# Early expert lists cut at three, five and seven counted groups, and weight stores as a task of their own

## The chip, the cores and the metric

The kernel runs on one core of a Trainium2 chip. The metric is the device time of one execution in microseconds (us). The core has five engines, each with its own queue in program order: TensorE (PE, its weight loads PEld), VectorE (DVE), ScalarE (ACT), GpSimd (POOL) and SyncE (SP), which here only issues DMAs. "Granted clock" is the share of full speed that TensorE was given, as the profile shows it.

## The reference

Three layers follow each other on 14336 tokens of 192 numbers (4 sequences of 3584).

```
out = sum over k of softmax(weight)[h, k] * x[t - 6 + k]        # 8 heads of 24, 7 taps
# first mixture: only tokens with out @ w_skip > 0
e = argmax(out @ w_gate);  g = softmax(out @ w_gate)[e]
x1 = out + g * (relu(out @ w1[e]) @ w2[e])                      # w1: 8 x 192 x 1024, w2: 8 x 1024 x 192
# second mixture: all tokens, a gate bias by modality
e2 = argmax(x1 @ w_gate2 + bias[modality]);  y = g2 * (relu(x1 @ w1b[e2]) @ w2b[e2])
```

The result is y. Each token goes through one expert of the first mixture or none, and one of the second.

## The kernel before, in words

**Phase 1** (`Phase1`, lines 669 to 840) makes the 7-tap sum and the gate scores. Tokens lie in 128 tiles of 112, in 8 groups of 16 tiles. A step v (line 821) does one head of one group's convolution, the transposes and gate matmuls of older pieces, and twice a *tick* of the task lists. `fin` (line 776) turns a group's scores into expert codes and metadata and stores the group's rows (values as two float16 halves) to `rows` in DRAM (line 805). There are 64 convolution steps and 12 more that finish.

**Counting and lists.** `route_a` (line 392) runs for each group when its codes are there: it counts tokens by expert (a scan `cuma`, a matmul with `tri` and `ones`, many small GpSimd operations), gives each token a place, and writes the token numbers of each place by one-hot matmuls (`oa`, `ob`). Each expert has `SB` = 7 blocks of 128 places. After `GA` = 4 groups the places of the first `EA` = 4 experts in `SA` = 3 blocks each are closed (line 434: the running base is raised to 3 * 128), and the sum so far is copied to the list `la` (line 484, index tile `idxa`). After 8 groups the list `ls` (`idxs`) is complete. Tokens beyond 7 blocks stay in `code` and are routed into 6 more blocks (`l1`), tokens of the second model that skip the first into list `lb` (`idxB`) and the rest into `l2`; that is `route` (line 585) with `ranks`, `qsl` and `invert`.

**Blocks.** `Ffn.run` (line 1017) goes through jobs. A block of 128 rows is gathered by GpSimd (an indirect DMA by the list), transposed by a DMA on SP, multiplied by the first weights (`mm1`, in two halves, into banks read by ScalarE as `hh` and by VectorE as `hlo`), and one job later by the second (`mm2`). Blocks of the first model add a residual (GpSimd, `xs`) and end in `x2a`/`x2s` on VectorE. `order` (line 1171) is: the first 12 blocks from `la` (experts 0 to 3, three each), then the rest of experts 1, 2, ..., 7, then 0, 44 blocks from `ls`; then 6 of `l1`. Jobs of the second model follow, mostly two to a set of weights.

**Weights.** `prep` (line 289) scales one expert's weights after another: squares of both matrices (before the first blocks by matmuls, later by ScalarE into `sa`), a sum over partitions by a matmul, a power of two `wsc`, then high halves by ScalarE and low halves by VectorE into `w1b`/`w2b` (first model, 3 buffers, `buf`) or into the one buffer `o` (second model), and stores to `s1a`, `s2a`, `s1b`, `s2b`. Two *lanes* (`LANES`, line 36) run it: lane 0 from phase 1 on, lane 1 from the time when phase 1's pools are given back (`late_pools`, line 1242). `guard` (line 1181) holds a scaling until its buffer is out of use (`step` at or beyond the last early or full block of expert e - 3, plus 2) or until `o` is free.

**What sets the order.** All work beside the blocks is written as Python generators; `yield n` means "go on in n ticks". `Tasks.tick` advances them, and `bg(i, pt)` (line 1301) calls it at four places of each block i: `tk` (counting and routes) twice while i < 12 and `ls` isn't ready, else once; `tkw` (the lanes) once; `tk2` (block maxima and scaling, `scale2`, line 942) once. While phase 1 has steps left, `bg` also does one. The order in which the generators issue is the order in each engine's queue, so a number after `yield` sets how far an instruction stands from what it waits for. At block 56 whatever is left in the lists is issued at once (`drain`).

Of the kernel before, what the change touches and what calls it, by code (L numbers as in the profile page):

```python
# [7 lines left out]
F32 = mybir.dt.float32  # L8
# [21 lines left out]
GA = 4  # L30
EA = 4
SA = 3
# [3 lines left out]
LANES = [(0, e) for e in range(E)] + [(1, 7)], [(1, e) for e in range(7)]  # L36
# [78 lines left out]
class Moe:  # L115
# [173 lines left out]
    def prep(self, ws, pool, pq, dst, guard, done, es, lane, lag, pace, free, busy, first, early):  # L289
# [22 lines left out]
        for n, (q, e) in enumerate(es):  # L312
            (wt, wr), w2t = nxt
            if early():
                for i, vs in enumerate(((wt,) * 8 + (wr[0:64],) * 8, (w2t,) * 12)):
                    for k, v in enumerate(vs):
                        c = k % 8 if i == 0 else k
                        v = v.bitcast(BF16)[:, c * 256 + 1:c * 256 + 256:2]
                        nc.tensor.matmul(g[:, i, :], v, v, start=(k == 0), stop=(k == len(vs) - 1))
                    yield 1  # L320
                yield 2
                dg = pq.tile([128, 512], F32, name="dg", bufs=1)[:, 0:256].rearrange("p (i c) -> p i c", i=2)
                nc.vector.tensor_tensor(dg, g, self.identf.unsqueeze(1).to_broadcast([128, 2, 128]), ALU.mult)
# [16 lines left out]
            yield 1  # L340
# [41 lines left out]
            yield 2 + q  # L382
            nc.sync.dma_start(ws[q][2][e], o1)
            yield 2 + q
            nc.sync.dma_start(ws[q][3][e], o2.bitcast(I32))
            yield 2 + q
            if q:
                free[0] = None
            if not last:
                yield max(1, lag() - 3 * (2 + q))  # L390

    def route_a(self, g, code, pool, ob, res):
# [41 lines left out]
        if g == GA - 1:  # L434
            nc.gpsimd.tensor_scalar(base[:, 0:EA], base[:, 0:EA], float(SA * 128), None, ALU.max)
# [47 lines left out]
        if g == GA - 1:  # L483
            self.finish("a", e, S, res["a"], 0)
# [4 lines left out]
    def finish(self, tag, ei, S, res, base, lp=None):  # L489
        nc = self.nc  # L490
        lp = lp or self.cp
        va = lp.tile([128, S], F32, name="va" + tag)
        nc.vector.tensor_scalar(va, ei, 0.0, None, ALU.is_gt)
        idx = lp.tile([128, S], I32, name="idx" + tag)
        if base:
            nc.vector.scalar_tensor_tensor(ei, va, float(base), ei, ALU.mult, ALU.add)
        nc.vector.tensor_scalar(idx, ei, 127.0, None, ALU.add)
        res.update(idx=idx, va=va)

    def ranks(self, code, pool, lag, r, wait=6):  # L500
# [6 lines left out]
        of = oh.rearrange("p c t -> p (c t)")  # L507
        nc.vector.tensor_tensor_scan(cum.rearrange("p c t -> p (c t)"), of, of, 0.0, ALU.add, ALU.max)
# [31 lines left out]
    def invert(self, S, q, sl, pool, ob, tag, res, lp, lag, base=0, val=None):  # L540
# [8 lines left out]
        for h in range(nb + 1):  # L549
            if h < nb:  # L550
# [5 lines left out]
                yield lag // 2  # L556
# [28 lines left out]
    def route(self, code, nst, tag, pool, ob, res, base=0, lag=1, S=None, np=0, lp=None, val=None):  # L585
# [49 lines left out]
        nc.vector.tensor_reduce(pos, cum.rearrange("p c t -> p t c"), AX.X, ALU.add)  # L635
        yield 1
# [32 lines left out]
class Phase1:  # L669
# [50 lines left out]
    def conv(self, g, h):  # L720
        nc, m = self.nc, self.m
        if h == 0:
            self.hl[g] = self.px.tile([TP, GT, RW], F16, name="hlx", bufs=1) if g == GA - 1 else self.p3.tile([TP, GT, RW], F16, name="hl", bufs=4)
# [119 lines left out]
class Ffn:  # L843
# [98 lines left out]
    def scale2(self, x2, mt, nb):  # L942
# [10 lines left out]
        yield 1  # L953
# [186 lines left out]
def build(tc, x, cw, m1w1, m1w2, mod, bias2, m2w1, m2w2, wgs, out):  # L1140
    with ExitStack() as ctx:
# [12 lines left out]
        la, ls, l1, lb, l2, lr = {}, {}, {}, {}, {}, {}  # L1154
# [25 lines left out]
        def lane(k):  # L1180
# [7 lines left out]

            return m.prep(ws, w["pw2"] if k else pw, pq, dst, guard, (d1, d2), LANES[k], k, lambda: 8 if k else 8 if late() else 14, lambda: 1 if late() else 3, owner, conv, 8 if k else 26, lambda: not late())

        def routes():
# [5 lines left out]
            while k < NSA:  # L1197
# [5 lines left out]
                k += n  # L1203
                yield 1
# [23 lines left out]
        while "idx" not in la:  # L1228
            if phase1() is None:
                tk.tick()  # L1230
# [11 lines left out]
        def late_pools():  # L1242
# [11 lines left out]
            tk.add(routes())  # L1254

# [36 lines left out]
        jobs = [mk(1, la if k < EA * SA else ls, e * SB + j, rows[0:GA * GT * 128 + 128, :] if k < EA * SA else rows, col=k, b=buf[e]) for k, (e, j) in enumerate(order)]  # L1292
# [8 lines left out]
        def bg(i, pt):  # L1301
# [35 lines left out]
            if i < n2:  # L1337
                for _ in range(2 if i < EA * SA and "idx" not in ls else 1):
# [71 lines left out]
```

## Time and profile before

| | us |
|---|---|
| median of 3 runs (lowest to highest) | 1015.85 (1015.10 to 1019.68) |
| profiled execution: time | 1015.87 |
| profiled execution: span of instructions | 1014.1 |
| PE busy | 929.5 (92%) |
| VectorE busy | 633.5 (62%) |
| GpSimd busy | 524.5 (52%) |
| ScalarE busy | 501.7 (49%) |
| mean granted clock of TensorE | 0.965 |

Busy time is the sum of instructions on an engine, so a share of 92% says nothing of where the other 8% are; the views by stage do. The first matmul of the first block runs at 139.79 us, the first matmul of the second model at 485.32 us. Times in rows are microseconds from the start of the span unless marked ns.

### The profile page before, as it was taken

The numbers are of one execution on the slowest core, as the hardware profiler recorded it, in microseconds if no ns is written. First come the engines' busy times: TensorE is split into PE (matmuls) and PEld (weight loads), VectorE is DVE, ScalarE is ACT, GpSimd is POOL, SyncE is SP. The second block draws the span as 40 slices with busy tenths as digits, with TensorE's granted clock in tenths as the row PEclk, the third lists the DMA queues.
The fourth block names the chain that finished last, engine by engine and source line by source line (L and its number), as shares of the span: only waits on it lengthen the run. The fifth ranks groups of instructions, "written<-read, shape, count | busy, mean of one in ns | idle before, by whom it ended". The sixth has DMA issues, their size and how long they took to land. (4 is left out here: it accounts for less than half of the span.)

```text
span 1014.1 us, 29393 instructions
## 1 busy us (share of the span) xinstructions
PE 929.5 (92%) x11174; PEld 865.0 (85%) x11174; DVE 633.5 (62%) x1716; ACT 501.7 (49%) x937; POOL 524.5 (52%) x1027
## 2 busy tenths in 40 slices
PE   5998969999898789998899999999999999999994
PEld 3666668899898789997799988998898999999994
DVE  5699976999989988983455555558633333333331
ACT  2786743656686555642455555543233333333331
POOL 4055788454344243334287776854355555555532
PEclk9999958999999899998999999999999999999997
DMA  8495778858899598579733334332275222233231
GB/s 292 147 319 204 238 237 210 228 177 219 232 251 264 129 304 241 170 240 259 257 81 108 98 88 117 99 112 67 55 257 164 72 76 73 74 75 75 74 96 47
DMA packets 109142, 165.49 MB, mean 163 GB/s; under 512 B 80975, under 2 KB 86073, under 8 KB 103232
## 3 DMA queue, kind: packets, MB, share of 16 engines
q1 hardware_dynamic: 94368, 134.02, 43.2%
q0 software_dynamic: 13920, 28.87, 12.0%
q8 instruction: 90, 1.47, 0.6%
q10 hardware_dynamic: 704, 0.63, 0.2%
q14 instruction: 60, 0.49, 0.2%
HBM read 181.56 MB, written 58.42 MB: 237 GB/s over the span
## 5 line engine op out<-in xcount | busy, mean ns | idle before, releaser
L70 PEld LDWEIGHTS <-w1b 128*128 128x128 f16 x4840 | 372.0, 99 | 40.3 <-issue 13.9
L70 DVE SCALAR_TENSOR_TENSOR ws<-bank,ws 128x512 f16<-128x512 f32 x220 | 151.9, 691 | 256.6 <-ACT ws L70 255.3
L70 PE MATMUL bank<-xp,w1b 128*128 128x256 f16 x2200 | 263.9, 273 | 4.3 <-DMA w1b<-s1b 2.6
L70 PE MATMUL bank<-w2b,ws 128*128 128x192 f16 x2640 | 239.1, 246 | 0.0
L70 PEld LDWEIGHTS <-ws 128*128 128x128 f16 (+2 forms) x2724 | 224.9, 98 | 2.3
L70 POOL DMA_INDIRECT out_dram<-u,si x114 | 115.2, 1011 | 167.8 <-ACT u L70 111.3
L70 ACT ACTIVATE ws<-bank 128x512 f16<-128x512 f32 x220 | 130.7, 597 | 119.5 <-PE bank L70 118.8
L70 PE MATMUL bank<-xt,w1b 128*128 128x128 f16 x2640 | 167.1, 223 | 10.4 <-DVE hlo L70 7.1
L70 PE MATMUL bank<-w2b,hh 128*128 128x192 f16 x1056 | 143.2, 252 | 4.6 <-DMA w2b<-s2a 4.6
L70 PE MATMUL bank<-w2b,hlo 128*128 128x192 f16 x528 | 132.8, 252 | 0.0
L70 ACT ACTIVATE hh<-bank 128x512 f16<-128x512 f32 x132 | 77.4, 591 | 103.4 <-PE bank L70 99.5
L70 DVE SCALAR_TENSOR_TENSOR hlo<-bank,hh 128x512 f16<-128x512 f32 x132 | 89.9, 685 | 49.8 <-ACT hh L70 49.5
L70 ACT ACTIVATE u<-bank,c 128x192 f32<-128x192 f32 x114 | 48.0, 421 | 146.5 <-PE bank L70 121.3
L70 POOL DMA_INDIRECT gt<-rows,idxs x44 | 50.0, 1136 | 131.8 <-issue 118.3
L70 PEld LDWEIGHTS <-hh 128*128 128x128 f16 x1056 | 97.3, 102 | 5.4 <-issue 4.8
L70 POOL DMA_INDIRECT gt<-rows,idx x64 | 63.5, 992 | 27.0 <-issue 15.0
L70 POOL DMA_INDIRECT gt<-rows,idxB x56 | 55.8, 997 | 27.3 <-issue 12.2
L70 PE MATMUL bank<-xg,band 128*112 128x384 f32 x128 | 58.8, 549 | 4.5 <-DVE hl L70 4.3
L70 POOL TENSOR_TENSOR xs<-gt 128x128 f32<-128x128 f16 x124 | 54.9, 467 | 5.5 <-DVE x2s L70 3.6
L70 PE MATMUL bank<-ob,oa 128*128 128x56 f16 (+2 forms) x446 | 50.0, 263 | 8.2 <-DVE ob L70 7.2
L70 ACT COPY xtb<-bank 128x672 f16<-128x672 f16 x64 | 46.0, 721 | 17.3 <-PE bank L70 17.0
L70 PEld LDWEIGHTS <-hlo 128*128 128x128 f16 x528 | 52.9, 100 | 0.3
(256 smaller groups left out, 1210.6 us busy)
## 6 DMA issues: line engine op xcount, KB each, us to landing
w1b<-s1b SPq DMA_DIRECT2D x59, 1024.0 KB
w2b<-s2b SPq DMA_DIRECT2D x59, 768.5 KB
ws<-in_moe_w_dram SPq DMA_DIRECT2D x16, 768.0 KB
xg<-in_x_dram SPq DMA_DIRECT2D x7, 1536.0 KB
rows<-hl SPq DMA_DIRECT2D x7, 1386.0 KB
ws<-in_moe_w_dram SPq DMA_DIRECT2D x16, 512.0 KB
ws<-in_moe_w_dram SPq DMA_DIRECT2D x32, 256.0 KB
s1a<-w1b SPq DMA_DIRECT2D x8, 1024.0 KB
```

What stands on the lines that cost most here:

```text
L70: r = f(*args, **kw)
```

## The change

The early list becomes three lists. `CUTS` names for each the groups counted and the range of blocks of an expert that it closes: after 3 groups blocks 0 and 1 of experts 0 to 2, after 5 groups blocks 2 and 3, after 7 groups blocks 4 and 5. So 18 blocks come first, six from each list, and of experts 1, 2 and 0 one block each is left for `ls`. Lane 0 scales expert 0 of the second model after expert 2 of the first; lane 1 has six experts. The two stores of a scaling become a generator `keep`, which after the start is a task of its own (`side`). Several `yield` numbers, the order of the squares, and the size of three VectorE operations (scan and two-part reduction) change. `tk` is ticked once a block's place while phase 1's pools live, twice from then to the last early list, then once.

```diff
-GA = 4
-EA = 4
-SA = 3
+CUTS = (3, 0, 2), (5, 2, 4), (7, 4, 6)
+EA = 3
+SA = CUTS[-1][2]
+NA = EA * SA
-LANES = [(0, e) for e in range(E)] + [(1, 7)], [(1, e) for e in range(7)]
+LANES = [(0, 0), (0, 1), (0, 2), (1, 0)] + [(0, e) for e in range(3, E)] + [(1, 7)], [(1, e) for e in range(1, 7)]
@@ prep
-                sa = pq.tile([128, 4], F32, name="sa", bufs=1)
-                for k, v in enumerate((wt, w2t[:, 0:4 * D], wr, w2t[:, 4 * D:])):
+                sa = pq.tile([128, 4], F32, name="sa", bufs=2)
+                for k, v in ((0, wt), (2, wr), (1, w2t[:, 0:4 * D]), (3, w2t[:, 4 * D:])):
...
-                    yield 2
+                    yield 2 if k < 3 else 5
...
             nc.vector.tensor_scalar(sc, sc, 2.0 ** 30, 2.0 ** FT, ALU.min, ALU.mult)
-            yield 1
+            yield 1 if early() else 3
...
-            yield 2 + q
-            nc.sync.dma_start(ws[q][2][e], o1)
-            yield 2 + q
-            nc.sync.dma_start(ws[q][3][e], o2.bitcast(I32))
-            yield 2 + q
-            if q:
-                free[0] = None
-            if not last:
-                yield max(1, lag() - 3 * (2 + q))
+            st = self.keep(ws, q, e, o1, o2, free)
+            if early():
+                for w in st:
+                    yield w
+                if not last:
+                    yield max(1, lag() - 3 * (2 + q))
+            else:
+                side.add(st)
+                if not last:
+                    yield 4
+    def keep(self, ws, q, e, o1, o2, free):
+        nc = self.nc
+        yield 2 + q
+        nc.sync.dma_start(ws[q][2][e], o1)
+        yield 2 + q
+        nc.sync.dma_start(ws[q][3][e], o2.bitcast(I32))
+        yield 2 + q
+        if q:
+            free[0] = None
@@ route_a
-        if g == GA - 1:
-            nc.gpsimd.tensor_scalar(base[:, 0:EA], base[:, 0:EA], float(SA * 128), None, ALU.max)
+        for n, _, b in CUTS:
+            if g == n - 1:
+                nc.gpsimd.tensor_scalar(base[:, 0:EA], base[:, 0:EA], float(b * 128), None, ALU.max)
...
-        if g == GA - 1:
-            self.finish("a", e, S, res["a"], 0)
+        for k, (n, _, _) in enumerate(CUTS):
+            if g == n - 1:
+                self.finish(f"a{k}", e, S, res["a"][k], 0, va=False)
@@ ranks
-    def ranks(self, code, pool, lag, r, wait=6):
+    def ranks(self, code, pool, lag, r, wait=4):
...
-        nc.vector.tensor_tensor_scan(cum.rearrange("p c t -> p (c t)"), of, of, 0.0, ALU.add, ALU.max)
+        for c in (0, 4):
+            of = oh[:, c:c + 4].rearrange("p c t -> p (c t)")
+            nc.vector.tensor_tensor_scan(cum[:, c:c + 4].rearrange("p c t -> p (c t)"), of, of, cum[:, 3, T - 1:T] if c else 0.0, ALU.add, ALU.max)
+            if not c:
+                yield 1
@@ invert
-                yield lag // 2
+                yield (lag - 1) // 2
@@ route
-        nc.vector.tensor_reduce(pos, cum.rearrange("p c t -> p t c"), AX.X, ALU.add)
-        yield 1
+        h = (T + 1) // 2
+        for a, b in ((0, h), (h, T)):
+            nc.vector.tensor_reduce(pos[:, a:b], cum[:, :, a:b].rearrange("p c t -> p t c"), AX.X, ALU.add)
+            yield 1
@@ scale2
         nc.vector.scalar_tensor_tensor(mt[:, :, 0], ef, 0.5, mt[:, :, 0], ALU.mult, ALU.mult)
-        yield 1
+        yield 4
@@ build
-        order = [(e, j) for e in range(EA) for j in range(SA)]
+        order = [(e, j) for _, a, b in CUTS for e in range(EA) for j in range(a, b)]
         order += [(e, j) for e in (*range(1, E), 0) for j in range(SA if e < EA else 0, SB)]
-        last = lambda e: max(i for i, o in enumerate(order) if o[0] == e and (e or i < SA))
+        last = lambda e: max(i for i, o in enumerate(order) if o[0] == e and (e or i < NA))
...
-        while "idx" not in la:
+        while "idx" not in la[0]:
...
+            tk2.add(kept())
...
-                for _ in range(2 if i < EA * SA and "idx" not in ls else 1):
+                for _ in range(2 if "x" in w and "idx" not in la[-1] else 1):
                     tk.tick()
```

`kept` is the copying of `va` for the complete list, taken out of `routes` and run in `tk2`. The jobs of an early list read `rows` only up to the groups it was counted from.

## Rows read from the trace of the kernel before

**Rows 1.** Busy time by stage: window, length, PE, PEld, DVE, ACT, POOL, clock, DMA, GB/s.
```profile
139.80:200.30 60.50, 52.49 (x634) 51.49 (x635) 43.81 (x113) 28.07 (x49) 42.85 (x118) 0.83 0.87 241
...
200.30:311.00 110.70, 104.53 (x1574) 103.68 (x1572) 100.50 (x273) 72.74 (x133) 49.09 (x92) 1.00 0.79 219
...
311.00:365.00 54.00, 41.73 (x565) 40.40 (x563) 52.32 (x141) 30.64 (x54) 19.32 (x34) 0.91 0.77 224
...
365.00:447.80 82.80, 81.23 (x1147) 80.94 (x1146) 71.35 (x173) 45.64 (x83) 34.83 (x67) 1.00 0.79 222
...
447.80:485.30 37.50, 29.96 (x409) 28.86 (x406) 17.59 (x46) 10.63 (x21) 12.84 (x24) 0.90 0.90 267
...
485.30:1014.00 528.70, 503.67 (x5558) 474.38 (x5558) 234.96 (x636) 222.11 (x442) 291.31 (x478) 0.99 0.37 102
```

**Rows 2.** Timeline of PE around the first block: start, length, operation, idle time before.
```profile
136.95 1.03 PE L70 MATMUL bank<-ob,oa 128*128 128x56 f16 x8 [1.22 <-DVE ob L70]
...
139.79 4.18 PE L70 MATMUL bank<-xt,w1b 128*128 128x128 f16 x40 [1.48 <-POOL genda L70]
...
147.87 0.59 PE L70 MATMUL bank<-cuma,tri 128*128 128x8 f32 x2 [3.90 <-DVE cuma L70]
```

**Rows 3.** Timeline of POOL from the fourth list to the last count.
```profile
123.56 0.46 POOL L70 TENSOR_TENSOR cuma<-cuma,oha 128x128 f32<-128x128 f32 x1
...
129.25 1.21 POOL L70 DMA_INDIRECT gt<-rows,idxa  x1 [0.19 <-issue]
...
173.10 0.22 POOL L70 TENSOR_TENSOR code<-code,oka 128x16 f32<-128x16 f32 x1
```

**Rows 4.** Timeline of SP, 158 to 172 us; last, its waits there (total, times, longest).
```profile
162.54 0.33 SPq L805 DMA_DIRECT2D rows<-hl  x1
...
169.18 0.34 SPq L296 DMA_DIRECT2D ws<-in_moe_w_dram  x1
...
SPq L296 <- DMA rows<-hl: 3.4, 1, 3.4
```

**Rows 5.** Timeline of DVE: results of blocks 0, 9 and 29.
```profile
160.00 0.41 DVE L70 SCALAR_TENSOR_TENSOR x2a<-bank,c,xs 128x192 f32<-128x192 f32 x1
...
213.56 0.42 DVE L70 SCALAR_TENSOR_TENSOR x2a<-bank,c,xs 128x192 f32<-128x192 f32 x1
...
311.18 0.42 DVE L70 SCALAR_TENSOR_TENSOR x2s<-bank,c,xs 128x192 f32<-128x192 f32 x1
```

**Rows 6.** Waits of PE over the whole span (total us, times, longest).
```profile
PE bank L70 <- ACT dg L70: 7.7, 4, 4.0
...
PE bank L70 <- DVE wsc L70: 4.3, 4, 1.9
```

**Rows 7.** Timeline of DVE in the second list's routing; last, all low halves in `o`.
```profile
318.45 2.29 DVE L70 TENSOR_TENSOR_SCAN rC<-rA 128x1024 f32<-128x1024 f32 x1
...
343.28 1.90 DVE L70 TENSOR_REDUCE pos<-rC 128x128 f32<-128x1024 f32 x1
...
L70 DVE SCALAR_TENSOR_TENSOR o<-ws,wsc,o x64: 604/742/1218, 192.0 to 440.5; 128x512 f16<-128x512 f32 x32, 128x384 f16<-128x384 f32 x32
```

**Rows 8.** Timelines at the hand-over: PE, SP and POOL.
```profile
458.05 2.40 PE L70 MATMUL bank<-xt,w1b 128*128 128x128 f16 x40
...
462.26 2.40 PE L70 MATMUL bank<-xt,w1b 128*128 128x128 f16 x40
...
472.86 0.48 PE L70 MATMUL bank<-w2b,hh 128*128 128x192 f16 x2 [3.99 <-DMA w2b<-s2a]
...
485.32 3.80 PE L70 MATMUL bank<-xp,w1b 128*128 128x256 f16 x20 [2.55 <-DMA w1b<-s1b]
...
447.83 0.36 SPq L866 DMA_DIRECT2D w1b<-s1a  x1
...
467.91 0.36 SPq L867 DMA_DIRECT2D w2b<-s2a  x1
...
455.82 0.94 POOL L70 DMA_INDIRECT gt<-rows,idxB  x1 [6.97 <-DVE idxB L70]
```

More of the change, by code (lines that the diff above doesn't have):

```diff
@@ L287, in pow2, with prep @@
         nc.vector.tensor_scalar(out.bitcast(I32), out.bitcast(I32), EXPM, None, ALU.bitwise_and)
-    def prep(self, ws, pool, pq, dst, guard, done, es, lane, lag, pace, free, busy, first, early):
+    def prep(self, ws, pool, pq, dst, guard, done, es, lane, lag, pace, free, busy, first, early, side):
         nc = self.nc
@@ L487, in route_a, with finish @@
         yield 1
-    def finish(self, tag, ei, S, res, base, lp=None):
+    def finish(self, tag, ei, S, res, base, lp=None, va=True):
         nc = self.nc
         lp = lp or self.cp
-        va = lp.tile([128, S], F32, name="va" + tag)
-        nc.vector.tensor_scalar(va, ei, 0.0, None, ALU.is_gt)
+        if va:
+            va = lp.tile([128, S], F32, name="va" + tag)
+            nc.vector.tensor_scalar(va, ei, 0.0, None, ALU.is_gt)
         idx = lp.tile([128, S], I32, name="idx" + tag)
@@ L722, in conv @@
         if h == 0:
-            self.hl[g] = self.px.tile([TP, GT, RW], F16, name="hlx", bufs=1) if g == GA - 1 else self.p3.tile([TP, GT, RW], F16, name="hl", bufs=4)
+            self.hl[g] = self.px.tile([TP, GT, RW], F16, name="hlx", bufs=1) if g == 3 else self.p3.tile([TP, GT, RW], F16, name="hl", bufs=4)
         if (g, h) not in self.pc:
@@ L1153, in build @@
         pq = ctx.enter_context(tc.tile_pool(name="pq", bufs=4))
-        la, ls, l1, lb, l2, lr = {}, {}, {}, {}, {}, {}
+        la, ls, l1, lb, l2, lr = [{} for _ in CUTS], {}, {}, {}, {}, {}
         ra = dict(a=la, s=ls)
@@ L1187, in guard, with kept @@
                 return False
-            return m.prep(ws, w["pw2"] if k else pw, pq, dst, guard, (d1, d2), LANES[k], k, lambda: 8 if k else 8 if late() else 14, lambda: 1 if late() else 3, owner, conv, 8 if k else 26, lambda: not late())
-        def routes():
+            return m.prep(ws, w["pw2"] if k else pw, pq, dst, guard, (d1, d2), LANES[k], k, lambda: 8 if k else 8 if late() else 14, lambda: 1 if late() else 3, owner, conv, 8 if k else 26, lambda: not late(), tkw)
+        def kept():
             while "idx" not in ls:
@@ L1203, in routes @@
                 k += n
+                yield 2
+        def routes():
+            while "idx" not in ls:
                 yield 1
@@ L1290, in mk @@
             return Job(size=size, part=part, kind=kind, l=l, j=j, src=src, col=col, b=b, s1=None if s is None else s1[s], s2=None if s is None else s2[s])
-        jobs = [mk(1, la if k < EA * SA else ls, e * SB + j, rows[0:GA * GT * 128 + 128, :] if k < EA * SA else rows, col=k, b=buf[e]) for k, (e, j) in enumerate(order)]
+        jobs = []
+        for k, (e, j) in enumerate(order):
+            c = [i for i, (_, a, b) in enumerate(CUTS) if k < NA and a <= j < b]
+            jobs.append(mk(1, la[c[0]], e * SB + j, rows[0:CUTS[c[0]][0] * GT * 128 + 128, :], col=k, b=buf[e]) if c else mk(1, ls, e * SB + j, rows, col=k, b=buf[e]))
         for k in range(NSA - SB + SA, NSA):
```

1 line of the change is left out of this document (removed).

## The prediction

> **What bounds the kernel now.** I read the busy time by stage first [rows 1]. From 485.3 us on TensorE is busy 503.67 of 528.7 us and the first model's change can hardly touch it; from 365 to 447.8 us it is busy 81.23 of 82.8 us. What it loses lies in three places. From 139.8 to 200.3 us it is busy 52.49 of 60.5 us, and its granted clock is 0.83, so some of that busy time is at the lower of its two levels (1.2 instead of 2.4 GHz). From 311 to 365 us it is busy 41.73 of 54 us, and there VectorE has no room: 52.32 of 54. From 447.8 to 485.3 us it is busy 29.96 of 37.5 us.
>
> The three have different limits. In the first, TensorE's queue, which runs in program order, stands behind the counting of the last groups: block 0's first matmul runs at 139.79, after a counting matmul that waited for `ob`, and then nothing until 147.87, where a counting matmul (`tri`) waits 3.90 us for `cuma` [rows 2]. Those counts in turn come from a long row of small GpSimd operations, which goes on to the last group's `code` at 173.10 [rows 3]. In the second, VectorE sets the pace (lists of the second model, scaling of two lanes of weights, the low halves of the hidden layer). In the third, weights of the next experts arrive late: 3.99 us and 2.55 us [rows 8].
>
> **The change, part by part.** *The start.* Before, the run of blocks begins when four groups are counted; the list is written about two phase-1 steps after the last convolution step. After, the list of three groups is there by step 57, so the run begins right after step 64, two steps earlier. The first two gathers then stand ahead of a chain of small operations on GpSimd: that engine ends the work before it at 123.56 + 0.46 = 124.0, while the first gather ran at 129.25 [rows 3]. The transposes gain less, because the store of group 5 is still ahead of them on SP. Block 0's matmuls now go ahead of the last two steps, and I put them at about 137 instead of 139.79. More comes from the ticks: a block advances the counting tasks by 3 steps in four places, not 4, until the steps of phase 1 are used up, and then by 1 until the late pools exist, not 2. By counting yields, the seventh group's `tri` matmul moves from block 0 to behind block 1's first layer and the last count from block 5 to block 8. So the wait of 3.90 us [rows 2] has a block in front of it, and block 0's result, written at 160.00 [rows 5], should be there at about 150.
>
> What is late next is GpSimd. From 124 to 174 us it ran the two groups' chains (some 44 us of work by the rows from 123.56 to 173.10 [rows 3]) and eight gathers; by the same point of the chain the new order puts two more gathers and two more residuals on it, 2 us each: it gets there at about 174 to 176, but that is now block 5, not block 3. Block 5 followed at 172 to 176 instead of 191, and block 9 (written at 213.56 [rows 5]) at 4.2 to 5 us a block at 193 to 195: 19 us early.
>
> One wait is new, and it takes back some. Lane 0 now scales expert 0 of the second model at once when the late pools exist (block 3), into `o`, which lies where phase 1's pools were. Before, the first write of `o` came at 192.0 [rows 7], far from them. What a reuse of that memory costs is seen on SP: the store of the last group is issued at 162.54, and lane 1's first load, issued at 169.18, waited 3.4 us for it [rows 4]. So a first write of `o` straight behind that store waits some 6.6 us. It stands on VectorE (the factor in `o2`) and ScalarE (the first copy); behind it on both is the hidden layer of blocks 4 and 5, and TensorE has about 2.4 + 2.2 us of matmuls that don't need it. Bounds: 0, if the freed piece is another one, and 9 us, if the store itself is late; I take 5. The start is then worth 14 us at block 9 (bounds 5 and 20).
>
> The Trainium skill (TensorE: Matmul & The Clock Gate, Architectural detail) says that the queues of ScalarE and VectorE are strictly first in, first out; by it the whole 6.6 us holds everything behind, and the trace agrees in kind: in four places TensorE waited 7.7 us for squares that stood behind another wait on ScalarE [rows 6].
>
> *What is left to do behind block 9.* The list of all groups comes at block 9 instead of 5, the next routing starts at block 9 instead of 7, and lane 0 must wait for block 15 before it scales expert 3, since buffer 0 stays in use for the early blocks. By then lane 0 has done experts 2 and (second model) 0, lane 1 none; before, they had done 2, 3 and 0. So one scaling is still owed: 8 operations of `o`'s kind, 4 x 0.74 + 4 x 0.60 = 5.4 us [rows 7], and about two blocks of the route's start, the scan of 2.29 us and one of its comparisons: some 8.5 us of VectorE's time. VectorE is busy 100.50 of 110.7 us from 200.3 to 311 and full from 311 to 365 [rows 1], and blocks 9 to 29 take (311.18 - 213.56) / 20 = 4.88 us each [rows 5]. Bounds 0 (it all falls where TensorE is the limit) and 10; since the nearest stretch is nine tenths full I take 7. The lanes themselves keep their length (28 steps each instead of 27 and 29), but the stores no longer stand in it; the lanes come out half a period apart.
>
> *Fewer holds in the queues.* Squares now come 5 steps before their matmul, the scale 3 steps before its use, the block maxima 4 steps before ScalarE's scaling; the scan of 2.29 us and the reduction of 1.90 us [rows 7] are cut in two. The waits for squares and scale are 7.7 + 4.3 us [rows 6], but the longest, 4.0 and 1.9, lie in the stretch where VectorE is full, and there the wait turns into one for the hidden layer. Of the other 6.1 us I count 2 (bounds 0 and 5). Cutting an operation adds its start again, a fraction of 1 us in all.
>
> *The hand-over to the second model.* Two things change. The list `idxB` was ready only when all tasks were drained at block 56: its first gather runs at 455.82, and SP holds `w2b`'s load until 467.91 behind a transpose of such rows, before the wait of 3.99 us [rows 8]. After, inversion takes 3 steps a round instead of 4, and the list is there at block 51. That may give 4 us. Against it: buffer 1 is now kept by expert 7 up to block 54 (before, block 51), so six sets of weights, not five, must come while the last eight blocks run at 462.26 - 458.05 = 4.21 us each [rows 8]. Five sets less the last `w2b` (4.57 sets) took from 447.83 to 485.32, 8.2 us each; 5.57 sets from a start 4.2 us earlier end 4.0 us later. Bounds -4 and +4; I take 0.
>
> The Trainium skill (DMA: Bandwidth & Descriptors, Where 436 GB/s comes from) gives about 358 GB/s from HBM for a core; a set of 1.84 MB would then come in an estimated 5.1 us, and the hand-over would gain. The trace moved 267 GB/s there [rows 1], and the sum goes by that.
>
> *Nothing:* the number of blocks. By the reference's inputs expert 0 has 444 and 625 tokens at the second and third cut for 512 and 768 places, so empty places are added, but it ends at 893 of 896, and the remainder list stays as it is. The copy of `va` and the early lists' own operations are under 0.5 us each and off the path.
>
> **Sum.** -14 (start) + 7 (work owed) - 2 (holds) + 0 (hand-over) = -9. The profiled execution took 1015.87 us (span 1014.1), as good as the median of 1015.85: 1007 us. Its own range by these bounds is 1001 to 1012.
>
> **Rivals.**
> 1. *The whole start is kept.* `o` doesn't wait, and the work owed falls into TensorE's stretches: -20 + 2 - 2 = 996. For it: ScalarE and VectorE are idle in the first stretch (VectorE 43.81 of 60.5 [rows 1]). Against it: the wait of SP on that same memory [rows 4].
> 2. *Paid back.* VectorE's total is what lasts from block 9 to 55; the early blocks run earlier, but the stretch of 311 to 365 grows, or the later lists come no sooner than before because GpSimd's chain is no shorter: -8 + 10 - 0 + 0, near 1016, no change. For it: 52.32 of 54 us.
> 3. *Slower: the new wait at `o`.* The last group's store hangs on GpSimd, which is the fullest engine there. If its two metadata copies come behind the queue of gathers and residuals, at 170 instead of 163, the store lands at about 177; VectorE and ScalarE stand from block 3's end until then, TensorE stops after 5 us, starts again at the low clock, and block 9 is where it was, 213. With the work owed: 0 + 7 - 2 + 2 = 1023. It decides from a landing later than about 175. Against it: fewer steps a block leave GpSimd more time for each.
>
> **How the numbers follow.** Forecast 0.43, rival 1 0.21, rival 2 0.21, rival 3 0.15. A measurement of this kernel tells 0.5% (5 us) from no change. Faster by more: nearly all of the forecast (0.41) and rival 1: 0.62. Within: rival 2 and the forecast's upper end: 0.22. Slower: rival 3 and rival 2's tail: 0.16. The range from 993 to 1021 takes in rivals 1 and 2.
>
> **What would show it.** Block 0's result near 150 and block 9's near 200 (213.56 before); no wait of TensorE for `cuma` over 2 us. A wait of VectorE or ScalarE at the first `o` for the store of `hl`, some 5 us long, about 162 us. Blocks 9 to 29 at 5.0 to 5.3 us each. `idxB` gathered without a wait, six weight loads from block 54's end, and TensorE still waiting for `w1b` or `w2b` there, 4 to 10 us in all. The forecast is wrong if block 9 is not at least 8 us earlier, if blocks 29 to 36 lose more than the 12 us they lose now, or if the hand-over loses over 12 us.

## The result, and the profile after

| | before | after |
|---|---|---|
| median of 6 runs (lowest to highest), us | 1016.82 (1015.10 to 1019.68) | 1029.24 (1027.38 to 1033.46) |
| ratio, 95% interval | | 1.0116 [1.0094, 1.0139] |
| profiled execution: span, us | 1014.1 | 1031.7 |

The change makes the kernel 1.2% slower, 12 us by the medians, where 9 us faster was forecast. In the profiled executions the difference is 17.6 us; the one after is the slowest of its six.

Busy time by stage after, in the windows of [rows 1] and with its columns:

```profile
139.80:200.30 60.50, 46.61 (x594) 45.60 (x592) 40.76 (x104) 25.97 (x48) 44.28 (x113) 0.82 0.79 226
200.30:311.00 110.70, 102.13 (x1518) 100.96 (x1516) 99.33 (x272) 70.25 (x128) 50.18 (x97) 1.00 0.73 206
311.00:365.00 54.00, 42.59 (x539) 41.38 (x537) 52.30 (x144) 30.07 (x53) 17.61 (x35) 0.89 0.62 184
365.00:447.80 82.80, 81.00 (x1103) 80.47 (x1101) 72.54 (x178) 48.47 (x84) 30.39 (x56) 0.97 0.76 224
447.80:485.30 37.50, 30.39 (x435) 29.80 (x434) 17.15 (x44) 11.08 (x22) 16.90 (x34) 0.97 0.91 235
...
172.00:186.00 14.00, 4.38 (x47) 4.25 (x45) 7.57 (x17) 4.32 (x7) 4.95 (x12) 0.63 0.89 234
```

TensorE is busy 5.9 us less in the first stage than before, though that stage was to gain. The last row shows where: from 172 to 186 us it is busy 4.38 of 14 us, and its granted clock is 0.63, a mean between its levels of 1.2 and 2.4 GHz. In the other four rows TensorE's busy time is within 2.4 us of the same row before.

What TensorE stands for is read by following three queues. PE's timeline (answers to [rows 2]), then SP's and GpSimd's (answer to [rows 4] and [rows 3]):

```profile
140.78 2.29 PE L71 MATMUL bank<-xt,w1b 128*128 128x128 f16 x20
...
149.21 1.28 PE L71 MATMUL bank<-xt,w1b 128*128 128x128 f16 x20 [2.11 <-DVE hlo L71]
151.50 0.51 PE L71 MATMUL bank<-cuma,tri 128*128 128x8 f32 x2 [1.02 <-DVE cuma L71]
...
171.47 1.28 PE L71 MATMUL bank<-xt,w1b 128*128 128x128 f16 x20
180.73 1.03 PE L71 MATMUL bank<-ob,oa 128*128 128x56 f16 x8 [7.98 <-ACT offa L71]
```
```profile
169.55 0.33 SPq L825 DMA_DIRECT2D rows<-hl  x1
...
176.81 0.34 SPq L297 DMA_DIRECT2D ws<-in_moe_w_dram  x1
```
```profile
167.06 1.07 POOL L71 DMA_INDIRECT gt<-rows,idxa  x1 [0.17 <-issue]
168.16 0.91 POOL L71 TENSOR_TENSOR xs<-gt 128x128 f32<-128x128 f16 x2
...
169.16 0.20 POOL L71 COPY hl<-gt 112x16 f32<-112x16 f32 x1
...
180.82 0.22 POOL L71 TENSOR_TENSOR cnta<-offa 128x16 f32<-128x16 f32 x1 [8.53 <-ACT offa L71]
```

And ScalarE's and VectorE's timelines in the same stretch:

```profile
164.36 0.60 ACT L71 ACTIVATE hh<-bank 128x512 f16<-128x512 f32 x1 [0.52 <-PE bank L71]
176.86 1.15 ACT L71 ACTIVATE o<-ws,wsc 128x1024 f16<-128x1024 f32 x1 [11.90 <-DMA rows<-hl]
177.91 0.58 ACT L71 ACTIVATE hh<-bank 128x512 f16<-128x512 f32 x1
...
180.52 0.16 ACT L71 COPY offa<-bank 128x16 f32<-128x16 f32 x1
```
```profile
166.46 0.35 DVE L71 RECIPROCAL gt<-gsm 112x32 f32<-112x32 f32 x1
...
168.90 0.26 DVE L71 SCALAR_TENSOR_TENSOR kf<-wsc 128x1 f32<-128x1 f32 x1
176.87 0.15 DVE L71 TENSOR_SCALAR o<-kf 128x1 int32<-128x1 int32 x1 [7.72 <-DMA rows<-hl]
178.52 0.69 DVE L71 SCALAR_TENSOR_TENSOR hlo<-bank,hh 128x512 f16<-128x512 f32 x1 [1.49 <-ACT hh L71]
```

GpSimd copies the last metadata of the last group into `hl` from 169.16 on, behind a gather and a residual; SP issues that group's store at 169.55 (162.54 in [rows 4]). That gather and residual are not what makes it late. What is copied, the gate values in `gt` (written from `gsm`), leaves VectorE at 166.81, and in the kernel before it left at 159.97:

```profile
159.62 0.35 DVE L70 RECIPROCAL gt<-gsm 112x32 f32<-112x32 f32 x1
```
```profile
162.01 0.33 POOL L70 COPY hl<-gt 112x16 f32<-112x16 f32 x1
```

From `gt` to the copy it is 2.35 us after and 2.04 us before. So 6.8 of the 7 us arise earlier, in the last group's own gate work.

Lane 0 has been ready to write since 165: its first writes into `o` wait on ScalarE for 11.90 us and on VectorE for 7.72 us, both until 176.87. Behind them stand the hidden layer of the next blocks (`hh`, `hlo`) and the counting copy `offa`. TensorE runs out of work at 172.75 and waits 7.98 us for that `offa`, and GpSimd's next count, `cnta`, 8.53 us for the same copy.

VectorE's results of blocks 0, 3, 9 and 29 after, the first, third and fourth of which answer to [rows 5]:

```profile
157.43 0.42 DVE L71 SCALAR_TENSOR_TENSOR x2a<-bank,c,xs 128x192 f32<-128x192 f32 x1
...
184.00 0.41 DVE L71 SCALAR_TENSOR_TENSOR x2a<-bank,c,xs 128x192 f32<-128x192 f32 x1
...
217.74 0.41 DVE L71 SCALAR_TENSOR_TENSOR x2a<-bank,c,xs 128x192 f32<-128x192 f32 x1
```

Block 29's is written at 322.7 us (311.18 before). These writes turned out to be a coarse clock: in the two traces they come 0.1 to 12.5 us behind TensorE (12.5 us for block 3 after, in the stall). A steadier one is the end of a block's second layer on TensorE (the end of each sixteenth matmul of the form `bank<-w2b,hh`):

| end of block's second layer, us | 0 | 3 | 5 | 9 | 29 | 36 | 55 | 61 | end of span |
|---|---|---|---|---|---|---|---|---|---|
| before | 158.8 | 177.2 | 190.7 | 209.7 | 309.8 | 352.2 | 453.9 | 491.0 | 1014.1 |
| after | 155.7 | 171.6 | 194.0 | 215.4 | 317.8 | 368.9 | 468.2 | 508.2 | 1031.7 |
| after, less before | -3.1 | -5.6 | +3.3 | +5.7 | +8.0 | +16.7 | +14.3 | +17.2 | +17.6 |

Up to block 3 the changed kernel leads by 5.6 us. It loses 8.9 us between blocks 3 and 5, 8.7 us between 29 and 36, and 2.9 us at the hand-over.

### The profile page after: what moved, and what is told of

Its sections match the earlier page's. It is cut to its first block, busy times and chain, and to the rows that moved or that the text cites. A ratio compares the mean times of both kernels' runs of the same rounds, so it can differ in the third digit from the quotient of the medians.

```text
span 1031.7 us, 29426 instructions
## 1 busy us (share of the span) xinstructions
PE 934.2 (91%) x11174; PEld 871.0 (84%) x11174; DVE 634.0 (61%) x1723; ACT 502.9 (49%) x937; POOL 528.8 (51%) x1033
## 5 line engine op out<-in xcount | busy, mean ns | idle before, releaser
L71 PE MATMUL bank<-xt,w1b 128*128 128x128 f16 x2640 | 169.2, 225 | 18.8 <-DVE hlo L71 12.7
L71 POOL DMA_INDIRECT gt<-rows,idxs x38 | 40.1, 1055 | 128.9 <-issue 105.8
L71 PEld LDWEIGHTS <-oa 128*128 128x128 f16 x446 | 45.0, 151 | 25.3 <-issue 13.7
L71 POOL DMA_INDIRECT gt<-rows,idxB x56 | 56.3, 1005 | 16.1 <-issue 10.2
```

What stands on the lines that cost most here:

```text
L71: r = f(*args, **kw)
```

## Experiments

**Both kernels once more, on one chip**, one execution of each:

> The kernel before once more, for a trace on the same chip as the next three: block 9 at 213 and block 55 at 454 as before if the chips differ only behind the hand-over.

> The changed kernel once more, for a trace on the same chip: waits of VectorE and ScalarE at the first `o` for the store of `hl` as before (7.7 and 11.9 us), block 9 some 4 us behind the kernel before.

Measured: 1012.31 and 1029.91 us. The pattern repeats: -5.1, +3.7, +5.9, +8.2 and +13.3 us at blocks 3, 5, 9, 29 and 36, with waits of 7.6 and 11.8 us at `o`. So it belongs to the schedule, not to one execution. The two traces of the kernel before differ by 0.3 us at block 9, 2.1 us at block 36 and 3.0 us at block 61; smaller differences than these say nothing there.

**The wait at `o` taken away.** Lane 0 scales into `o` only from step 6 on, after the store has landed:

```diff
-                if "o" in w and owner[0] in (None, k):
+                if "o" in w and owner[0] in (None, k) and step[0] >= 6:
```

> The changed kernel, but the scaling into `o` may only begin from block 6 on (2.5 blocks later); nothing else moves. Theory 1 (VectorE and ScalarE stand at the first write of `o` for the store of the last group, 7.7 and 11.9 us in the changed kernel's trace, and that is most of the loss): no such wait, result of block 3 at about 173 instead of 184, block 9 at about 208 instead of 217.7, total about 1019, some 9 to 10 us below the changed kernel. Theory 2 (what is owed behind the early blocks costs the 12 us, the wait only fills time that would be lost anyway): blocks 0 to 9 earlier, the rest falls back, total 1026 to 1030.

Measured: 1.0005 [0.9979, 1.0031] of the kernel before. The slowdown of 1.0116 is gone, so the wait costs about 1.1%, 11 us. (Ratios here and below compare with runs of the kernel before made together with them, whose medians lie between 1016.16 and 1025.84 us. From block 61 to the end the kernel before takes 523.1 us in its trace and this version 530.3 us in its own, though the change does not touch that part, so traces are compared up to block 61.) Windows of this kernel, with the columns of [rows 1] (compare the row from 172 of the changed kernel above):

```profile
140.00:156.00 16.00, 13.28 (x140) 12.62 (x138) 12.46 (x33) 6.25 (x13) 14.00 (x36) 0.67 0.88 278
156.00:172.00 16.00, 15.50 (x218) 15.33 (x216) 12.82 (x36) 4.38 (x10) 13.19 (x43) 1.00 0.59 155
172.00:186.00 14.00, 13.14 (x186) 12.88 (x185) 7.85 (x22) 7.46 (x13) 10.77 (x30) 1.00 0.90 226
...
139.64:156.30 16.66, 13.94 (x152) 13.28 (x150) 13.00 (x34) 6.85 (x14) 14.66 (x37) 0.67 0.86 273
156.30:203.40 47.10, 44.30 (x621) 43.58 (x619) 37.04 (x93) 22.47 (x42) 33.81 (x89) 1.00 0.80 216
```

From 172 to 186 us TensorE is now busy 13.14 us instead of 4.38, at a granted clock of 1.00. Its second layers end at 154.6, 180.7, 203.0, 306.7, 355.2, 450.5 and 492.9 us (blocks 0, 5, 9, 29, 36, 55, 61): block 9 comes 12.4 us before that of the changed kernel, but only 6.7 us before that of the kernel before. So the wait is the whole slowdown against the kernel before, but not the whole miss of the forecast: without the wait the rest of the change gains nothing, where the forecast's terms without it come to -14 us.

**The wait put into the kernel before.** Two tiny writes into `o`, one on VectorE and one on ScalarE, right behind the last group's store; nothing else is changed:

```diff
+            def touch():
+                nc.vector.memset(o[1][:, W2C:].bitcast(I32), 0)
+                nc.scalar.copy(o[0][:, 0, 0:16], m.ident[:, 0:16])
+                yield 1
+            tk2.add(touch())
```

> The kernel before with two small writes into `o` right behind the issue of the last group's store: four bytes a partition by VectorE, 16 numbers by ScalarE; they are overwritten later. Nothing else is changed. Theory 1: both engines stand there for the store's 6 to 7 us, TensorE runs out of work after some 5 us, and part of it is made up, since VectorE has idle time before block 9: ratio 1.004 to 1.010, block 5 at 198 to 203 instead of 191. Theory 2 (a wait there is hidden by TensorE's other work): 1.000 to 1.003.

Measured: 1.0036 [1.0014, 1.0057], between the two theories. The writes on VectorE and ScalarE, and SP's store and the first load behind it:

```profile
168.41 0.06 DVE L70 MEMSET o<- 128x1 int32 x1 [6.94 <-issue]
```
```profile
168.37 0.20 ACT L70 COPY o<-ident 128x16 f16<-128x16 f16 x1 [9.97 <-issue]
```
```profile
161.67 0.33 SPq L805 DMA_DIRECT2D rows<-hl  x1
...
168.32 0.34 SPq L296 DMA_DIRECT2D ws<-in_moe_w_dram  x1
```

The profile names no releaser of the two writes ("issue"); but both start when the load does, 6.7 us after the store. A like wait, 0.8 and 1.9 us shorter on the two engines and 8.5 us earlier, costs 3.7 us in this schedule and 11 us in the changed one. Here TensorE loses 5.0 us up to block 3 (182.2 against 177.2), of which 2.6 us show at block 5 (193.3 against 190.7); there the wait takes away 13.3 us at block 5 (194.0 against 180.7).

**Another piece of memory for the last group.** One unused `hl` buffer is asked for first, so that the last group's store reads another of the four:

```diff
+        self.p3.tile([TP, GT, RW], F16, name="hl", bufs=4)
```

> The changed kernel with one tile that is never used asked for ahead of phase 1's `hl` buffers, so that the last group uses the fourth buffer and not the third; no instruction is added, taken away or moved. Theory 1 (the wait is the reuse of that one piece of memory by `o`, and it is most of the loss): the waits at `o` go, block 3 at about 172 instead of 184, ratio to the kernel before 0.998 to 1.003. Theory 2 (any write into the freed memory waits for the whole pool's last reader): wait and ratio stay as they are, 1.010 to 1.013.

Measured: 1.0106 [1.0084, 1.0128], no change. Its waits from 155 to 215 us:

```profile
ACT o L71 <- DMA rows<-hl: 11.9, 1, 11.9
...
DVE o L71 <- DMA rows<-hl: 7.7, 1, 7.7
```

So it isn't that one buffer lying under `o`. Whether the wait covers all the memory of the closed pool, or `o` overlaps the other buffer too, stays open.

**ScalarE's next wait.** With the wait at `o` gone, ScalarE stands 3.94 us at 179.49 for the squares of lane 1's first weights (`dg<-ws`). The first of two runs on it moved the squares of lane 0 and so missed: that wait belongs to lane 1, whose loads SP issues only when the store has landed.

```diff
-                    yield 4
+                    yield 12 if (q, e) == (1, 0) else 4
```

> The changed kernel with the scaling into `o` held until block 6, and lane 0's next squares 8 steps (2 blocks) later, since lane 0 must wait for block 15 anyway. Theory A (ScalarE's 3.94 us wait for the weight load at 179 us holds the hidden layer behind it and costs the start some of its 19 us): block 5 at 181 to 183 instead of 185.6, block 9 at 200 to 202, ratio 0.995 to 1.000. Theory B (VectorE's work behind block 9 takes back whatever the start gains): block 9 earlier, ratio 0.999 to 1.003.

Measured: 1.0031 [1.0012, 1.005], and blocks 5 and 9 end within 0.2 us of the version with the hold alone on TensorE. The second run gave lane 1 more steps ahead of its squares (16 instead of 8; the 26 in the text on record is lane 0's number):

```diff
-            return m.prep(... conv, 8 if k else 26, ...)
+            return m.prep(... conv, 16 if k else 26, ...)
```

> The changed kernel without the early block at the new `o` wait (the hold until the first expert's step 6), and lane 1 of the weight loads starts with 16 steps of its own instead of 26, its first squares so that they are asked for later than the loads can land. Theory A: ScalarE's 4.5 us of waiting at 179.5 us for lane 1's first loads costs the start; with it gone block 5 ends at 181 to 183 us instead of 185.6, block 9 at 199 to 201 instead of 203.4, and the ratio to the kernel before is 0.995 to 1.000. Theory B: the wait lies beside TensorE's own backlog of scaling and transposes; block 9 stays at 202 to 205 and the ratio at 0.999 to 1.003, like the version with the hold alone.

Measured: 0.9995 [0.9972, 1.0018]. ScalarE's wait is gone; what stood behind it runs at once:

```profile
179.01 0.60 ACT L71 ACTIVATE hh<-bank 128x512 f16<-128x512 f32 x1 [2.17 <-DVE x2a L71]
179.50 1.14 ACT L71 ACTIVATE o<-ws,wsc 128x1024 f16<-128x1024 f32 x1
```

Yet block 9 ends at 204.1 us on TensorE, no earlier (203.0). That is theory B: with the hold alone TensorE is busy 44.30 of the 47.10 us between the results of blocks 0 and 9, as the last row of the hold's windows shows, so nothing beside it is worth much there.

**The parts alone, on the kernel before.** Only the three early lists (and the copy of `va` as a task):

```diff
-GA = 4
-EA = 4
-SA = 3
+CUTS = (3, 0, 2), (5, 2, 4), (7, 4, 6)
+EA = 3
...
```

> The kernel before with the three early lists (18 early blocks, `va` copied in a task of its own) and nothing else: lanes, number of ticks, yields, sizes and stores as before. Theory 1: the lists by themselves start the blocks earlier and no write of `o` meets the store: 1008 to 1016. Theory 2: expert 3's buffer is held until block 15, so scaling crowds later, and the lists alone already lose: 1021 to 1027.

Only the yields, the order of the squares and the split operations, the stores still in line:

```diff
-                    yield 2
+                    yield 2 if k < 3 else 5
...
-            yield 1
+            yield 1 if early() else 3
...
```

> The kernel before with only the new yield numbers, the new order of the squares, and the scan and the reduction cut in two; lists, lanes, ticks and stores as before. Theory 1: the 2 us that the prediction counted for fewer holds, total 1013 to 1017. Theory 2: the route's rounds of 3 steps instead of 4 make VectorE's stretch denser and the matmuls wait for `ob` (4.5 and 3.5 us in the changed kernel, 0.2 before): 1019 to 1024.

The same with the stores as a task of their own:

```diff
+                side.add(st)
+                if not last:
+                    yield 4
...
```

> The kernel before with the yields and the stores as a task of their own; lists, lanes and ticks as before. Yields without the stores' task measured 1.019. Theory A (a scaling's chain grew to 32 steps with stores in line, so weights came late; with the task it is 28 and they come in time): ratio 0.996 to 1.003, no wait of TensorE for `w1b` written by VectorE or ScalarE. Theory B (the denser route itself costs): 1.010 or more.

Only the fewer ticks while phase 1 runs:

```diff
-                for _ in range(2 if i < EA * SA and "idx" not in ls else 1):
+                for _ in range(2 if "x" in w and "idx" not in ls else 1):
```

> The kernel before with only the fewer ticks: the counting is ticked once a block's place while phase 1's pools live, then twice until the complete list is ready. Lists, lanes, yields, stores as before. Theory A (the fewer ticks bring the start's 10 us, the lists only make room for them): waits for `cuma` below 2 us, block 9 at 203 to 207 instead of 213.6, then paid back in part by the later routing: ratio 0.992 to 1.000. Theory B (without the early lists the complete list comes too late or the start is no earlier): block 9 at 210 or later, ratio 1.000 to 1.008.

Measured: 1.0189 [1.0139, 1.0239], 1.0193 [1.0157, 1.0229], 1.0089 [1.0059, 1.012] and 1.0009 [0.9997, 1.0022].

The lists alone lose more than either theory allowed, and bring no earlier start: block 5 ends at 192.9 us on TensorE (190.7 before) and block 9 at 213.0 (209.7). From block 29 to 36 they take 48.8 us instead of 42.4. TensorE waits 4.6 us there for `w1b` from VectorE (200 to 510 us; none before), which points to the crowded scaling of theory 2; it was not tested further.

The yields alone lose more than their theories allowed, too. The yields without the side task make a scaling's chain longer than the time that an expert's blocks take; the weights then come too late. Waits of TensorE from 200 to 510 us in that version (total, times, longest):

```profile
PE bank L70 <- DVE hlo L70: 16.2, 6, 10.0
PE bank L70 <- DVE w1b L70: 5.6, 2, 5.0
...
PE bank L70 <- ACT w1b L70: 1.8, 1, 1.8
```

TensorE waits there for `w1b` straight from the engines that scale it, which the kernel before never does in that stretch. Taking the stores out of the chain gives back 1%, and none of these waits for `w1b` is left; the ratio of 1.0089 lies between the two theories. The fewer ticks alone lower TensorE's waits for `cuma` at the start (139 to 205 us) from 5.2 to 1.4 us and bring the end of block 5 7.8 us earlier and that of block 36 10.3 us earlier (341.9 against 352.2), and at block 61 there is next to nothing left of it (490.5 against 491.0): 5.9 us go between blocks 36 and 45, where VectorE is busy 53.20 of 58.3 us.

**The parts taken out of the version with the hold.** First the ticks as before:

```diff
-                for _ in range(2 if "x" in w and "idx" not in la[-1] else 1):
+                for _ in range(2 if i < NA and "idx" not in ls else 1):
```

> The changed kernel with the scaling into `o` held until block 6 (no wait there), and the counting ticked as often as before (twice a place until the complete list is ready). Theory A (fewer steps a block are what starts the blocks earlier: with more of them TensorE stands behind the counts again): waits of TensorE for `cuma` and `ob` of 5 us and more before 200 us, block 9 at 208 to 215 instead of 203, ratio to the kernel before 1.004 to 1.010. Theory B (the early lists by themselves do it): block 9 stays at 203, ratio 0.998 to 1.003.

then all yields, the order of squares and the split operations as before, the side task kept:

> The changed kernel with the scaling into `o` held until block 6, and all yields, the order of the squares, the scan and the reduction as in the kernel before; lists, lanes, ticks and the stores' own task stay. Theory A (the yields hide waits worth some 2 to 5 us): ratio to the kernel before 1.002 to 1.006, with TensorE's waits for squares (`dg`) back. Theory B (the yields are worth nothing, VectorE is what is full): 0.998 to 1.002. Theory C (they cost: the denser route and the longer chain of a scaling): 0.992 to 0.998.

and the lanes as before in the changed kernel itself, which also keeps lane 0 away from `o` at the start:

```diff
-LANES = [(0, 0), (0, 1), (0, 2), (1, 0)] + [(0, e) for e in range(3, E)] + [(1, 7)], [(1, e) for e in range(1, 7)]
+LANES = [(0, e) for e in range(E)] + [(1, 7)], [(1, e) for e in range(7)]
```

> The changed kernel with the two lanes' experts as in the kernel before: lane 1 scales expert 0 of the second model first, lane 0 goes from expert 2 to expert 3 of the first. Theory 1: lane 1's squares put the first write of `o` some blocks behind the store, so no wait there, total 1017 to 1021. Theory 2: with one scaling less done by block 9 (lane 0 waits for block 15 anyway) the later stretches get denser, total 1026 or more.

Measured: 1.0054 [1.0024, 1.0083], 1.0106 [1.0072, 1.0139] and 1.0082 [1.0061, 1.0103]. Against 1.0005 with all parts and the hold, each part is worth 0.5 to 1%; for the ticks the two intervals overlap. With the ticks as before, block 0 ends at 162.6 us on TensorE instead of 154.6 and block 9 at 215.1 instead of 203.0, and TensorE waits for `cuma` again (139 to 205 us; total, times, longest):

```profile
PE bank L71 <- DVE cuma L71: 7.3, 2, 6.7
```

That is theory A: the earlier start comes from the fewer ticks. With the yields as before, the ratio is above all three theories, and waits for squares are back, of which the version with the hold has none from 200 to 510 us:

```profile
PE bank L71 <- ACT dg L71: 10.2, 7, 2.5
```

So the yields, which cost 0.9% on the old schedule with the stores as a task of their own, pay here. Old lanes do avoid the wait (block 9 at 203.0 us on TensorE), and lose it again behind block 29 (497.3 at block 61 against 492.9); their ratio lies between the two theories.

**The hand-over.** In the version with the hold, expert 0's last block before expert 7, and the remainder's buffers to match, so that five sets come at the end and not six:

```diff
-        order += [(e, j) for e in (*range(1, E), 0) for j in range(SA if e < EA else 0, SB)]
+        order += [(e, j) for e in (*range(1, E - 1), 0, E - 1) for j in range(SA if e < EA else 0, SB)]
...
```

> The changed kernel with the scaling into `o` held until block 6, and the last block of expert 0 put before expert 7's blocks, the remainder's buffers in the order 0, 2, 1: buffer 2 is free early, so five sets of weights, not six, must come in the last eight blocks, as in the kernel before. Theory A (the sixth set costs the hand-over 4 to 5 us): blocks 55 to 61 in 37 to 39 us instead of 42, ratio to the kernel before 0.994 to 0.998. Theory B (the hand-over is bound by the order of SP's queue or by transposes, not by the sixth set): 40 us or more there, ratio 0.999 to 1.003.

Measured: 1.0056 [1.0029, 1.0084]. Blocks 55 to 61 take 37.4 us instead of 42.3, as before the change (37.1), so with six sets this stretch is some 5 us longer, as theory A has it. But the time isn't won, it moves: blocks 45 to 55 take 52.0 us instead of 45.2. A load now stands ahead of transposes there, and TensorE waits for one:

```profile
433.85 4.43 PE L71 MATMUL bank<-xt,w1b 128*128 128x128 f16 x40 [4.99 <-DMA xt<-gt]
```

No version that was run beats the kernel before: the best three are level with it (0.9995, 1.0005, 1.0009).

## Why the prediction was wrong

**The step that failed** is the first term of the sum, "-14 (start)". By TensorE it measured +5.7 us at block 9, and both of its parts were mis-sized: the lead, put at 19 us, is 6.7 us when the wait is taken away, and the new wait, put at 5 us, costs 12.4 us. So the missing lead weighs 12.3 us and the wait 7.4 us. By VectorE's results, which the forecast went by, it is 8.9 and 9.3 us (217.74 after, 203.42 with the hold, 213.56 before).

**The wait.** "So a first write of `o` straight behind that store waits some 6.6 us. ... Bounds: 0, if the freed piece is another one, and 9 us, if the store itself is late; I take 5." The mechanism and its place were right, the size was not: 12.4 us at block 9 by TensorE (215.4 against 203.0 with the hold), 11 us of the total, above the upper bound. Two things were left out. The store was taken from [rows 4], 162.54; it came at 169.55. And the price was taken below the wait itself, since TensorE had "about 2.4 + 2.2 us of matmuls that don't need it". ScalarE had been waiting since 165, and `offa` behind it holds the counting, so GpSimd and TensorE both stood until 180.7; TensorE, whose block 3 ended at 171.55, ran out of work at 172.75. Its granted clock over that stretch was 0.63 (1.00 with the hold). The rule of strict queues that the prediction cites from the Trainium skill (TensorE: Matmul & The Clock Gate, Architectural detail) would have had the whole wait hold everything behind it; here the trace agrees, with 7.72 and 11.90 us.

Rival 3 described what happened, near its numbers: metadata copies "at 170 instead of 163" (169.16), landing "at about 177" (176.87), "the low clock", "block 9 is where it was, 213" (217.74), 1023 us (1029.24). It had 0.15 because "fewer steps a block leave GpSimd more time for each". The reason that it gives for the late copies, the gathers and residuals ahead of them, covers little: from 139.8 to 172.75 us GpSimd is busy 27.76 us (28.38 before), and the copies are late because `gt` is. No single part of the change makes the store late: it is issued at 163.22 with the lists alone, at 167.63 with the fewer ticks alone, and at 166.40 in the version with the hold and the ticks as before (168.52 with the hold alone).

The terms side by side, by TensorE's ends of second layers (us, plus is later than before):

| term | forecast | after | with the hold |
|---|---|---|---|
| start to block 9 | -14 (-19 without the wait) | +5.7 | -6.7 |
| work owed, blocks 9 to 36 | +7 | +11.0 | +9.7 |
| blocks 36 to 61, with the hand-over | 0 | +0.5 | -1.2 |
| sum to block 61 | -7 | +17.2 | +1.8 |

The 2 us for fewer holds have no place of their own in this table; the forecast's sum with them is -9.

**The lead** is 6.7 us without the wait, not 19 (numbers of the version with the hold). The forecast took GpSimd for the next limit. Its last count comes at 178.66 us, not far from the 174 to 176 of the forecast, but between the results of blocks 0 and 9 GpSimd is busy 33.81 and TensorE 44.30 of 47.10 us, 4.9 us a block: TensorE sets the pace. Block 0's second layer ends at 154.6 us, and its result is written at 156.3, not 150. Its first matmul runs at 139.64, not 137, and TensorE is busy 13.94 us at a granted clock of 0.67 up to that result, for which the forecast has no term. From there block 9 at 193 to 195 was no likely value but a floor: from 139.64 to 203.4 us TensorE is idle for 63.76 - 58.24 = 5.5 us, and 13.94 x (1 - 0.67) = 4.6 us is an estimate of what the lower clock costs. Without either, 193.3. Part of the 19 was also never lead: before, block 9's result was written at 213.56, 3.9 us after TensorE had finished it.

**The work owed** was undersized but near its upper bound (7 forecast, bounds 0 and 10; 11.0 us after, 7.4 us in the second pair of traces, 9.7 us with the hold), and half right in cause. Most of it falls where VectorE is full, between blocks 29 and 36. Three windows, each from about the end of block 29 to that of block 36, of before, after and with the hold:

```profile
309.50:351.90 42.40, 33.32 (x463) 32.41 (x461) 40.90 (x115) 25.54 (x46) 14.67 (x26) 0.92 0.71 205
```
```profile
317.60:368.40 50.80, 39.39 (x475) 38.11 (x473) 49.47 (x140) 25.78 (x46) 15.55 (x31) 0.87 0.60 177
```
```profile
306.20:354.70 48.50, 36.78 (x480) 35.57 (x478) 47.37 (x133) 26.37 (x47) 16.00 (x32) 0.93 0.67 184
```

VectorE (the fifth number) has 8.6 and 6.5 us more to do there, and the stretch is 8.4 and 6.1 us longer. One part is the scaling that the forecast counted: between the ends of blocks 0 and 9 VectorE writes 16 low halves before, 9 after and 8 with the hold, and between those of blocks 29 and 36 it writes 14, 20 and 18, 4.3 and 2.8 us more than before. The other part is not the route's start. The scan of the second list comes at block 29 with the hold, and came at block 32 before (318.45 in [rows 7]), so its one-hot operations (`oa`, `ob`), none of which ran in this stretch before, take 4.3 us of VectorE's time here (4.7 after). The scan's first half with the hold, and the `oa` group of this stretch (count, busy us and mean ns):

```profile
304.45 1.22 DVE L71 TENSOR_TENSOR_SCAN rC<-rA 128x512 f32<-128x512 f32 x1
```
```profile
L71 DVE TENSOR_TENSOR oa<-iq,q 128x1024 f16<-128x1024 f16 x3 | 2.1, 691 | 0.0
```

A VectorE that is full there and grows is rival 2's mechanism, and it took the early lead of the version with the hold whole.

**The holds in the queues** were put at 2 us. Within the new schedule the yields are worth more, 1% by the run without them, in which TensorE waits 10.2 us for squares; on the old schedule they cost 0.9%. The forecast had priced only the waits that [rows 6] show for the kernel before, and 2.3 of the 6.1 us that it counted from lie in phase 1 (at 46, 88 and 130 us), where the new numbers do not apply.

**The hand-over** came out as costed, near 0: the +0.5 and -1.2 us from block 36 to 61 are less than the two traces of the kernel before differ by. The list `idxB` is there at 444.2 us, and the first gather by it, at 461.9, doesn't wait. Six sets come instead of five, and TensorE waits for weights and for rows there:

```profile
476.60 0.33 PE L71 MATMUL bank<-w2b,hh 128*128 128x192 f16 x2 [1.84 <-DMA w2b<-s2a]
482.48 4.02 PE L71 MATMUL bank<-xt,w1b 128*128 128x128 f16 x40 [3.74 <-DMA xt<-gt]
...
502.26 3.59 PE L71 MATMUL bank<-xp,w1b 128*128 128x256 f16 x20 [2.22 <-DMA w1b<-s1b]
```

The second model's first matmul comes at 502.26 us, 16.9 us later than in [rows 8], and only 0.6 us more are lost behind it. From the load of first weights at 456.80 us to that matmul, six sets less the last `w2b` (5.57 sets) take 45.46 us, 8.2 us each, as the forecast put it; three of the loads are issued 6.6 us apart (473.98, 480.65 and 487.21). The 5.1 us that the prediction estimated from the Trainium skill (DMA: Bandwidth & Descriptors, Where 436 GB/s comes from) were not reached here.

**Smaller slips of the prediction**, none of which decides: the first write of `o` before is ScalarE's at 190.86 us (192.0 in [rows 7] is the first low half); of the four waits for squares two, 6.3 of 7.7 us, stood behind a wait of ScalarE, the others behind its own work; rival 2's sum is +2, so 1018 and not 1016; and all its bounds together reach from -29 to +9 us, 987 to 1025, not 1001 to 1012.

What stays open: why the last group's gate work, and with it the store, comes 7 us later; what the lists alone lose 1.9% by; and which limit puts block 61 back at 490.5 us in the run with the fewer ticks alone, which reaches block 36 10.3 us early.

## What to carry to other kernels

In these runs memory that a closed pool gives back was not free until the last DMA out of it had landed (waits of 7.72 and 11.90 us). Before moving a first write there ahead in an in-order queue, take the landing from the new order (follow the store's producer back, engine by engine), and charge it to every engine behind the write. Read a lead off the engine that bounds the time, not off results that another engine writes. And follow an early gain to the next stretch where another engine is full: here VectorE, with 6.5 to 8.6 us more to do in one stretch, took all of it.

## What was not expected of the hardware

A wait of some 7 us on VectorE (10 to 12 us on ScalarE) costs 3.7 us in one order and 11 us in another. The store of a group's rows (1.42 MB) holds the freed memory for 6.6 to 7.3 us from its issue, by the next load into that memory: 161.67 to 168.32, 162.54 to 169.18, 169.55 to 176.81.
